# Where the second sums of a pair of groups are kept, and the order of one period's transposes, splits and scaling

## The chip, the cores and the metric

The kernel runs on one core of a Trainium2 chip. The metric is the device time of one execution in microseconds (us). Before the change three runs gave 612.68, 611.83 and 611.43 us, a median of 611.83. TensorE is called PE here, VectorE DVE, ScalarE ACT, GpSimd POOL and SyncE SP, as in the profile.

## The reference

Retention (4 batches, 8 heads, 768 steps, 64 wide) is followed by a feed-forward block with a gate:

```python
for t in range(S):
    state = gamma * state + einsum('bhd,bhe->bhde', k[:, :, t], v[:, :, t])
    y[:, :, t] = scale * einsum('bhd,bhde->bhe', q[:, :, t], state)
x = y.transpose(0, 2, 1, 3).reshape(3072, 512)
h = x @ w_in                      # 512 -> 2048
g = h * erf(softplus(h))
out = g @ w_out                   # 2048 -> 512
```

q, k, v and the output are float32; w_in and w_out come as 64-bit numbers, which the kernel converts itself.

## The kernel before, in words

**Precision.** A product x·w of the feed-forward block is made of three products in a faster format: x and w are each split into a high part, a low part and a difference (`split`, L328, and `split_weights`, L314: one ACT operation for the high part, then two DVE operations for `lo` and `dif`). The three products go to two sums in two PSUM banks, a (from hi and lo) and b (from dif), and the result is (1 + 1/Z)·a − b/Z.

**Groups, units, bricks.** The 3072 tokens are 12 groups of 256; a group is two chunks of 128 steps. The 2048 hidden columns are 16 strips of 128. A *unit* of `pair_unit` (L740) multiplies one strip for two neighbouring groups, g and g + 1: 8 matmuls into bank a, then 4 into bank b (L748), 512 columns each. The four banks of the pool `ps_o` serve two units in turn, so a unit's banks are those of the unit before the last. A unit's result, here called a *brick* (128 x 512 numbers, 256 KB), is *evacuated* by its `put` (L756): for most units `together` (L337), which is one ACT operation (L339) that copies a, scaled, into a small buffer h, and one DVE operation (L340) that adds b to it; then POOL starts the transfer of h to DRAM (`HID2`). For the units of g in `APART` (g = 1 and 2: 4 + 8 = 12 bricks) the two sums stay apart: ACT copies a to h (L760) and b to a second small buffer `low` (L761), and POOL transfers each on its own, `low` to `HID3` (L762) and h to `HID2` (L765). The small buffers (`b2`, L95) are six, shared by h, `low`, the masked scores `am` and the outputs y; large ones (`b4`, L92) are 34 of 4 KB a partition, shared by nearly everything else.

**Periods.** After a start in which groups 0 and 1 are made, the loop at L1052 runs periods g = 2 to 12. In period g PE runs the units of pair g − 1 (six units in period 2, eight afterwards), and the retention of chunks 2g + 2 and 2g + 3 is woven in. Two joins stand between units: `begin` (L577: scores and the chunks' own state updates, on PE) and `results` (L616: queries times states and scores times values, on PE, then ACT copies to xT at L651). Between them `states` (L595) masks the scores (L603, into `am`) and adds up the states (L614) on DVE. After `results`, `crossed_sums` (L654) makes four short DVE sums (L660, L662), and `split_x` (L664) makes x_hi on ACT (L331), x_lo and x_dif on DVE (L332, L333).

**Preparation.** The generator `prepare(j)` (L548) has five steps for the chunks j and j + 1: transpose the keys on DVE (L560), scale the queries on DVE (L555), transpose them (L560 again), and then twice scale the values of one chunk, 8 ACT operations (L567). Its first step is taken in the period before. SP loads the keys and queries for it in 16 pieces each (`load_pair`, L149, L163); POOL loads values and keys in another layout (L147, L157).

**Order.** Every engine works through its own list in order. The lists follow the dictionaries in `period` (L988): a unit's matmuls are issued, then what the dictionary has for that place, then the unit's `put`. In period 3 (g == G2 + 1, L1004) `begin` stands ahead of unit 3 and `results` ahead of unit 5. On ACT and DVE, place 0 has three steps of `prepare(8)` with `hi_of(2)` (the high part of weight piece 2) between; place 1 the split of piece 2, `hi_of(3)` and the fifth step; place 2 the split of piece 3; place 3 the states. Piece 2 is wanted by units 4 and 5, piece 3 by units 6 and 7.

**Last stage.** `project` (L940) multiplies the gated bricks with w_out: 48 steps of 24 matmuls (L957). Bricks are loaded back by `load_hidden` (L866) in transfers of 512 KB; of those whose sums are apart the second sums come in `low` buffers (L879) and are added on DVE (`add_lows`, L893). Softplus (L898) and erf (L902) run on ACT, the gate's product on DVE (L912). Half-groups that are apart are loaded one step earlier than the others (L1086, L1090).

Of the kernel before, what the change touches and what calls it, by code (L numbers as in the profile page):

```python
# [13 lines left out]
F32 = mybir.dt.float32  # L14
# [3 lines left out]
AF = mybir.ActivationFunctionType  # L18
# [3 lines left out]
P = 128  # L22
C = 128
JPC = 4
GT = 256
# [19 lines left out]
Z = 2.0**-12  # L45
# [4 lines left out]
def kernel(  # L50
# [13 lines left out]
    nc = tc.nc  # L64
# [7 lines left out]
    n_ft = d_ff // P  # L72
    NPC = n_ft // 2
    DH = d_model // 2
    FIRST = JPC // 2 - 1
# [10 lines left out]
    scratch = ctx.enter_context(tc.tile_pool(name="scratch", bufs=1, space=bass.MemoryType.DRAM))  # L86
# [5 lines left out]
    def b4(name, shape, dtype=F32):  # L92
        return big.tile([P] + shape, dtype, name=name, tag="b4")

    def b2(name, shape, dtype=F32):  # L95
        return small.tile([P] + shape, dtype, name=name, tag="b2")

    def b8(name, shape, dtype=F32):
# [4 lines left out]
    HID = {  # L103
        g: scratch.tile([P, n, GT], F32, name=f"hid{g}") for g, n in ALONE.items()
    }
    HID2 = {
        g: scratch.tile([P, n_ft // 2, 2, GT], F32, name=f"hids{g}") for g in range(FIRST, NG - 1)
    }

    APART = (FIRST, FIRST + 1)  # L110
    HID3 = {g: scratch.tile([P, n_ft // 2, 2, GT], F32, name=f"hidl{g}") for g in APART}
    XR = []
    WOF = [scratch.tile([P, 2, d_model], F32, name=f"wof{n}") for n in range(NPC)]

# [222 lines left out]
    def together(to, a, b):  # L337

        nc.scalar.activation(to, a, AF.Copy, scale=1 + 1 / Z)  # L339
        nc.vector.scalar_tensor_tensor(to, b, -1 / Z, to, op0=ALU.mult, op1=ALU.add)  # L340
# [29 lines left out]
    for r in range(2):  # L370
        own = slice(r * D, (r + 1) * D)
# [176 lines left out]
    def prepare(j):  # L548


        for name, store, x in (("k", KT, KB[j]), ("q", QT, QB[j])):
            if name == "q":
                own = x.rearrange("p u (a d) -> p u a d", d=32)
                scale = kq_b[:, 1, :, j % NC : j % NC + 2].rearrange("p u c a -> p u (c a)")
                nc.vector.tensor_tensor(  # L555
                    own, own, scale[:, :, :, None].to_broadcast([P, HP, 8, 32]), op=ALU.mult
                )
                yield
            t = b4(name + "T", [HP, 2 * C])
            nc.vector.transpose(t.rearrange("p u t -> p (u t)"), x.rearrange("p u t -> p (u t)"))  # L560
            for i in range(2):
                store[j + i] = t[:, :, i * C : (i + 1) * C]
            yield
        for i in range(2):
            for h in range(H):
                x = V[j + i][:, h]
                nc.scalar.activation(x, x, AF.Copy, scale=kq_s[:, (j + i) % NC, 0, h : h + 1])  # L567
            yield
# [167 lines left out]
    def place_of(g, of):  # L736

        return int(of % 3 > min(g % 3, (g + 1) % 3))

    def pair_unit(g, ft):  # L740

        a, b = banks(g == NG - 2)
        n, u = divmod(ft, 2)
        at = sorted((g % 3, (g + 1) % 3))
        at = slice(at[0], at[1] + 1, at[1] - at[0])
        for to, parts in ((a, (0, 1)), (b, (2,))):
            for kk, i in itertools.product(range(n_k), parts):
                nc.tensor.matmul(  # L748
                    to,
                    W[n][i][:, kk * 2 * P + u * P : kk * 2 * P + (u + 1) * P],  # L750
                    XR[i][:, at, kk],
                    start=(kk == 0 and i == parts[0]),
                    stop=(kk == n_k - 1 and i == parts[-1]),
                )

        def put():  # L756
            h = b2("h", [2, GT])
            if g in APART:
                low = b2("low", [2, GT])
                nc.scalar.activation(h, a, AF.Copy, scale=1 + 1 / Z)  # L760
                nc.scalar.activation(low, b, AF.Copy, scale=-1 / Z)  # L761
                nc.gpsimd.dma_start(HID3[g][:, ft % 8], low)  # L762
            else:
                together(h, a, b)
            nc.gpsimd.dma_start(HID2[g][:, ft % 8], h)  # L765

        return put
# [61 lines left out]

    pair = load_pair(JPC + 2)  # L830
    prep = prepare(JPC + 2)
    a, b = JPC, JPC + 1
    during = {
# [30 lines left out]
    HID_, LOWS, E, G, WO = {}, {}, {}, {}, {}  # L864

    def load_hidden(n):  # L866

        if n >= NG * NU:
            return
        HID_[n] = b4("hid", [4, GT])  # L870
        g, i = divmod(n, NU)
        of = g if g % 2 == i // 2 else g - 1
        LOWS[n] = []
        if FIRST <= of < NG - 1 and (of != 1 or i == 3):
            src = HID2[of][:, i % 2 * 4 : i % 2 * 4 + 4, place_of(of, g)]
            for f in range(2) if of in APART else ():
                LOWS[n].append(b2("low", [2, GT]))
                at = i % 2 * 4 + 2 * f
                nc.sync.dma_start(LOWS[n][f], HID3[of][:, at : at + 2, place_of(of, g)])  # L879
        else:  # L880
            at = i * 4 if g < 2 else i % 2 * 4
            src = HID[g][:, at : at + 4]
        nc.sync.dma_start(HID_[n], src)
# [101 lines left out]

    LOADS = {4: (3, 4, 5, 6), 5: range(2, 8), 6: (0, 1, 4, 5, 6, 7), 7: (2, 3, 4, 5), 8: (1, 2, 3, 4)}

    def period(g, prep, next_prep):  # L988

        a, b = 2 * g + 2, 2 * g + 3  # L990
        one, two = partial(partial, unit), partial(partial, pair_unit)
        if g == G2:
            units = [one(g, 4), one(g, 5)] + [two(1, ft) for ft in range(12, 16)]
            return units, joined(1, 4, g), {
                0: [(split_weights, 6)],
                1: [(states, a), (states, b), (hi_of, 7)],
                2: [(split_weights, 7), (hi_of, 0)],
                3: [(split_weights, 0), (hi_of, 1)],
                4: [(crossed_sums, a), (crossed_sums, b), (split_x, a, 2)],
                5: [(split_weights, 1), (steps, next_prep, 1)],  # L1000
            }, range(4)
        if g < NG:
            units = [two(g - 1, ft) for ft in range(8 - 8 * (g % 2), 16 - 8 * (g % 2))]
        if g == G2 + 1:  # L1004
            return units, joined(3, 5, g), {
                0: [(steps, prep, 2), (hi_of, 2), (steps, prep)],
                1: [(split_weights, 2), (hi_of, 3), (steps, prep)],
                2: [(split_weights, 3)],
                3: [(states, a), (states, b)],
                5: [(crossed_sums, a), (crossed_sums, b), (split_x, a, 2)],  # L1010
                7: [(steps, next_prep, 1)],
            }, range(4)
        if g < NG - 2:
            return units, joined(2, 5, g), {
                0: [(steps, prep, 4)],
                1: [(convert, 2)],
                2: [(states, a), (convert, 1)],
                3: [(states, b), (convert, 1)],
                4: [(convert, 2 if g < 8 else 1)],
                5: [(crossed_sums, a), (crossed_sums, b)],  # L1020
                6: [(split_x, a, 2)],
                7: [(steps, next_prep, 1 if g < NG - 3 else 4), (convert, 1)],
            }, LOADS.get(g, ())
        if g == NG - 2:
            return units, joined(1, 3, g), {
                0: [(steps, prep, 4), (load_w_out, 0)],
                1: [(states, a), (load_w_out, 1)],
                2: [(states, b), (split_w_out, 0)],
                3: [(crossed_sums, a), (crossed_sums, b)],
                4: [(split_w_out, 1), (load_hiddens, 0)],  # L1030
                5: [(split_x, a, 2)],
                6: [(softplus, 0), (load_w_out, 2)],
                7: [(erf, 0), (gated, 0)],
            }, ()
        if g == NG - 1:
            return units, {}, {
                0: [(split_g, 0), (split_w_out, 2), (load_w_out, 3)],
                1: [(split_g, 1), (load_hiddens, 1)],
                2: [(split_w_out, 3)],
                3: [(softplus, 1), (load_w_out, 4)],  # L1040
                4: [(erf, 1)],
                5: [(split_w_out, 4), (load_w_out, 5)],
                6: [(gated, 1)],
                7: [(split_g, 2), (load_hiddens, 2)],
            }, ()
        return [one(NG - 1, n) for n in range(NPC // 2, NPC)], {}, {
            0: [(split_w_out, 5), (load_w_out, 6)],
            1: [(split_g, 3), (load_w_out, 7)],
            2: [(split_w_out, 6)],
        }, ()  # L1050

    for g in range(G2, NG + 1):  # L1052
# [19 lines left out]
        prep = next_prep  # L1072
    split_w_out(7)

    for n in range(NG * NU):
        g, i = divmod(n, NU)
# [19 lines left out]
    for i in range(2):  # L1096
        at = slice(i * DH, (i + 1) * DH)
# [45 lines left out]
```

## Time and profile before

| | |
|---|---|
| median of three runs | 611.83 us |
| the profiled execution's own time | 612.2 us |
| its span, from first to last instruction | 610.5 us |
| granted TensorE clock | 0.999 |
| moved by DMA | 112.58 MB |

In the profile's rows the columns are as follows. The busy line has busy time, share of the span and number of instructions of each engine. A row of the windows view has the stretch, its length, then each engine's busy time and instructions, the granted clock, the mean share of 16 DMA engines that were busy, and GB/s. A row of the waits view has who waited, for whom, the total in us, how often and the longest. A row of a timeline has start and duration in us, engine, line, operation, the tiles written and read, shape, how many equal ones in a row, and in brackets how long the engine had been idle and what ended that. A row of groups has busy time and mean ns of one, then the idle time before and its enders. A row of the chain of work that ended last has start, duration, and what.

Period 3 begins near 100 us, the later ones follow every 26 us, and the last stage begins near 345 us.

### The profile page before, as it was taken

To read this page: it belongs to the slowest core of one execution; us is meant where nothing else is said; L and a number is where in the kernel's file an instruction comes from. 1 tells how busy PE (TensorE), PEld (TensorE's weight loads), DVE (VectorE), ACT (ScalarE), POOL (GpSimd) and SP (SyncE) were. 2 spreads that over 40 slices of the span, in tenths; PEclk is the share of its full clock that TensorE was granted. 3 is DMA by queue.
4 is the path that set the end of the run, shared out by engine and by line. 5 is a ranking of instruction groups with operands and counts; after the bars stand their busy time and mean duration, and the time that the engine had idled before them with its cause. 6 is when DMAs were issued, how large, how long until landed. Compare 5 with 4: busy or idle time off the path is not lost.

```text
span 610.5 us, 13200 instructions
## 1 busy us (share of the span) xinstructions
PE 602.3 (99%) x5190; PEld 504.7 (83%) x5190; DVE 461.4 (76%) x578; ACT 396.0 (65%) x625; POOL 138.8 (23%) x236
## 2 busy tenths in 40 slices
PE   8999999999999999999999999999999999999997
PEld 7888897888888888888888988888888888888885
DVE  5899897677978679787778986977877768668640
ACT  3684576474453634345486787889989888988910
POOL 1086545463526535241112200000000000000000
PEclk9999999999999999999999999999999999999999
DMA  9999689998979998894645865355424433531301
GB/s 203 313 257 280 169 170 276 284 252 241 223 198 272 279 269 169 253 231 151 225 152 183 288 205 177 100 172 173 130 74 141 144 98 104 172 124 48 105 34 35
DMA packets 148878, 112.58 MB, mean 184 GB/s; under 512 B 103376, under 2 KB 128208, under 8 KB 148816
## 3 DMA queue, kind: packets, MB, share of 16 engines
q1 hardware_dynamic: 132192, 61.24, 39.1%
q0 software_dynamic: 16064, 50.36, 25.9%
q8 instruction: 41, 0.67, 0.5%
q14 instruction: 21, 0.17, 0.1%
q10 hardware_dynamic: 560, 0.14, 0.1%
HBM read 72.89 MB, written 38.80 MB: 183 GB/s over the span
## 4 chain that ended last, share of the span: by engine, by line
PE 80%; DMA 9%; SPq 7%; DVE 2%; issue 1%; POOL 0%; DVEq 0%
PE o L748 29%; PE o L957 21%; PE r L957 11%; PE hp L957 11%; SPq L163 4%; DMA raw<-in_moe_w_in_dram 3%; DMA kb<-in_k_dram 2%; DMA qb<-in_q_dram 2%; SPq L199 2%; DMA hidl<-low 1%; PE o L721 1%; SPq L140 1%; PE hp L748 1%; PE r L748 1%; PE hp L583 1%
## 5 line engine op out<-in xcount | busy, mean ns | idle before, releaser
L748 PE MATMUL o<-x_hi,w_hi 128*128 128x512 f32 x288 | 114.3, 397 | 0.8 <-ACT h L760 0.8
L748 PE MATMUL o<-x_lo,w_lo 128*128 128x512 f32 x288 | 112.3, 390 | 0.3 <-DVE x_lo L332 0.3
L912 DVE TENSOR_TENSOR e<-hid,e 128x1024 f32<-128x1024 f32 x48 | 56.6, 1221 | 50.3 <-ACT e L902 50.2
L339 ACT ACTIVATE h<-o 128x512 f32<-128x512 f32 x64 | 37.7, 594 | 81.5 <-PE o L748 76.3
L748 PE MATMUL o<-x_dif,w_dif 128*128 128x512 f32 x288 | 77.0, 389 | 0.0
L765 POOL DMA_DIRECT2D hids<-h x76 | 41.9, 552 | 117.0 <-DVE h L340 110.0
L340 DVE SCALAR_TENSOR_TENSOR h<-o,h 128x512 f32<-128x512 f32 x64 | 43.7, 687 | 30.2 <-ACT h L339 27.5
L748 PEld LDWEIGHTS o<-x_hi,w_hi 128*128 128x128 f32 x288 | 54.0, 188 | 13.2 <-ACT h L760 1.2
L748 PEld LDWEIGHTS o<-x_lo,w_lo 128*128 128x128 f32 x288 | 54.1, 188 | 11.3 <-DVE x_lo L332 0.6
L748 PEld LDWEIGHTS o<-x_dif,w_dif 128*128 128x128 f32 x288 | 54.1, 188 | 11.2
L333 DVE SCALAR_TENSOR_TENSOR g_dif<-g_hi,g_lo 128x1024 fp32r<-128x1024 f32 x48 | 58.8, 1225 | 3.2
L331 ACT ACTIVATE g_hi<-e 128x1024 fp32r<-128x1024 f32 x48 | 51.0, 1062 | 15.6 <-DVE e L912 13.0
L332 DVE TENSOR_TENSOR g_lo<-e,g_hi 128x1024 fp32r<-128x1024 f32 x48 | 58.6, 1221 | 0.0
L898 ACT ACTIVATE e<-hid 128x1024 f32<-128x1024 f32 x48 | 48.5, 1053 | 4.2 <-DVE hid L893 2.9
L687 PE MATMUL hp<-xT,w 128*128 128x256 f32 x224 | 49.7, 381 | 0.0
L902 ACT ACTIVATE e<-e 128x1024 f32<-128x1024 f32 x48 | 48.2, 1052 | 0.3
L687 PEld LDWEIGHTS hp<-xT,w 128*128 128x128 f32 x224 | 42.1, 190 | 5.7
L957 PE MATMUL o<-w_hi,g_hi 128*128 128x512 f32 x120 | 46.7, 389 | 0.0
L957 PE MATMUL o<-w_lo,g_lo 128*128 128x512 f32 x120 | 46.7, 389 | 0.0
L957 PE MATMUL o<-w_dif,g_dif 128*128 128x512 f32 x120 | 46.7, 389 | 0.0
L567 ACT ACTIVATE v<-v,kq_s 128x64 f32<-128x64 f32 x144 | 35.6, 337 | 0.0
L898 ACT ACT_TABLE_LOAD x24 | 30.8, 1283 | 2.1 <-DMA hid<-hids 1.4
(208 smaller groups left out, 1274.9 us busy)
## 6 DMA issues: line engine op xcount, KB each, us to landing
hids<-h POOLq DMA_DIRECT2D x76, 256.0 KB, 4.2
hid<-hids SPq DMA_DIRECT2D x38, 512.0 KB, 5.4
raw<-in_moe_w_in_dram SPq DMA_DIRECT2D x32, 256.0 KB, 5.4
raw<-in_moe_w_out_dram POOLq DMA_DIRECT2D x32, 256.0 KB, 6.1
out_dram<-y SPq DMA_DIRECT2D x23, 256.0 KB, 2.1
hid<-hid SPq DMA_DIRECT2D x10, 512.0 KB, 5.2
kb<-in_k_dram SPq DMA_DIRECT2D x144, 32.0 KB, 3.3
v<-in_v_dram POOLq DMA_DIRECT2D x18, 256.0 KB, 6.4
```

The source lines that it names most:

```text
L331: nc.scalar.activation(hi, x, AF.Copy, scale=KEEP)
L332: nc.vector.tensor_tensor(lo, x, hi.bitcast(F32), op=ALU.subtract)
L333: nc.vector.scalar_tensor_tensor(dif, hi.bitcast(F32), Z, lo.bitcast(F32), op0=ALU.mult, op1=ALU.subtract)
L339: nc.scalar.activation(to, a, AF.Copy, scale=1 + 1 / Z)
L340: nc.vector.scalar_tensor_tensor(to, b, -1 / Z, to, op0=ALU.mult, op1=ALU.add)
L687: nc.tensor.matmul(HP_[bank][:, col], w[:, kk, ft % 2 * P : (ft % 2 + 1) * P], XC[g][:, kk], start=(kk == 0), stop=(kk == n_k - 1),)
L748: nc.tensor.matmul(to, W[n][i][:, kk * 2 * P + u * P : kk * 2 * P + (u + 1) * P], XR[i][:, at, kk], start=(kk == 0 and i == parts[0]), sto ...
L765: nc.gpsimd.dma_start(HID2[g][:, ft % 8], h)
L898: nc.scalar.activation(E[n], HID_[n], AF.Softplus)
L902: nc.scalar.activation(E[n], E[n], AF.Erf)
L912: nc.vector.tensor_tensor(E[n], HID_.pop(n), E[n], op=ALU.mult)
L957: nc.tensor.matmul(Y[g][t][x // 2], G[n][x][:, f, t * P : (t + 1) * P], W_OUT[ft // 2][x][:, ft % 2 * d_model : (ft % 2 + 1) * d_model], s ...
```

## The change

- `APART` holds only g = 1. Its four bricks (strips 12 to 15, made in period 2) put both sums in one large buffer of 4 KB a partition, which goes to DRAM in one transfer of 512 KB; `HID3` holds both sums side by side, and the last stage reads either from there.
- The eight units of g = 2 (period 3) are evacuated with `together`, like those of all later pairs; their bricks go to `HID2` and are loaded back without `low`.
- The values' scaling is a generator of its own, `values`. Only for j = 8 (`2 * JPC`) it is not the end of `prepare`, and in period 3 the order is: place 0: values of chunk 8, `hi_of(2)`; place 1: scaling and transpose of the queries, values of chunk 9; place 2: split of piece 2, `hi_of(3)`; place 3: the states, then the split of piece 3.

```diff
+    APART = (FIRST,)
+    HID3 = {g: scratch.tile([P, n_ft // 2, 2, 2, GT], F32, name=f"hid3_{g}") for g in APART}
     HID2 = {
         g: scratch.tile([P, n_ft // 2, 2, GT], F32, name=f"hids{g}") for g in range(FIRST, NG - 1)
+        if g not in APART
     }
-    APART = (FIRST, FIRST + 1)
-    HID3 = {g: scratch.tile([P, n_ft // 2, 2, GT], F32, name=f"hidl{g}") for g in APART}
...
+        if j != 2 * JPC:
+            yield from values(j)
+
+    def values(j):
         for i in range(2):
             for h in range(H):
                 x = V[j + i][:, h]
...
         def put():
+            if g in APART:
+                h = b4("h", [2, 2, GT])
+                nc.scalar.activation(h[:, 0], a, AF.Copy, scale=1 + 1 / Z)
+                nc.scalar.activation(h[:, 1], b, AF.Copy, scale=-1 / Z)
+                nc.gpsimd.dma_start(HID3[g][:, ft % 8], h)
+                return
             h = b2("h", [2, GT])
-            if g in APART:
-                low = b2("low", [2, GT])
-                nc.scalar.activation(h, a, AF.Copy, scale=1 + 1 / Z)
-                nc.scalar.activation(low, b, AF.Copy, scale=-1 / Z)
-                nc.gpsimd.dma_start(HID3[g][:, ft % 8], low)
-            else:
-                together(h, a, b)
+            together(h, a, b)
             nc.gpsimd.dma_start(HID2[g][:, ft % 8], h)
...
-            src = HID2[of][:, i % 2 * 4 : i % 2 * 4 + 4, place_of(of, g)]
+            four, own = slice(i % 2 * 4, i % 2 * 4 + 4), place_of(of, g)
+            src = HID3[of][:, four, 0, own] if of in APART else HID2[of][:, four, own]
...
-                nc.sync.dma_start(LOWS[n][f], HID3[of][:, at : at + 2, place_of(of, g)])
+                nc.sync.dma_start(LOWS[n][f], HID3[of][:, at : at + 2, 1, own])
...
+    vals = values(2 * JPC)
...
-                0: [(steps, prep, 2), (hi_of, 2), (steps, prep)],
-                1: [(split_weights, 2), (hi_of, 3), (steps, prep)],
-                2: [(split_weights, 3)],
-                3: [(states, a), (states, b)],
+                0: [(steps, vals), (hi_of, 2)],
+                1: [(steps, prep, 2), (steps, vals)],
+                2: [(split_weights, 2), (hi_of, 3)],
+                3: [(states, a), (states, b), (split_weights, 3)],
```

## The prediction, made before the result was known

> **What bounds the kernel now.** I read the page's busy line first, then the windows view, then who PE waited for.
>
> ```profile
> PE 602.3 (99%) x5190; PEld 504.7 (83%) x5190; DVE 461.4 (76%) x578; ACT 396.0 (65%) x625; POOL 138.8 (23%) x236
> ```
> ```profile
> 0.00:20.00 20.00, 17.07 (x208) 14.82 (x210) 12.90 (x28) 8.18 (x18) 2.44 (x15) 1.00 1.06 209
> 95.00:105.00 10.00, 8.94 (x38) 6.84 (x37) 5.65 (x8) 7.42 (x20) 4.59 (x8) 1.00 0.89 260
> 120.00:500.00 380.00, 380.00 (x3298) 316.77 (x3297) 299.46 (x368) 253.03 (x388) 83.08 (x134) 1.00 0.67 191
> 500.00:610.50 110.50, 106.46 (x470) 87.83 (x468) 63.58 (x59) 73.77 (x73) 0.00 (x0) 0.99 0.30 96
> ```
> ```profile
> PE o L748 <- ACT h L760: 0.8, 1, 0.8
> PE o L748 <- DVE x_lo L332: 0.3, 1, 0.3
> PE r L632 <- DVE state L614: 0.2, 1, 0.2
> ```
>
> TensorE bounds it. Of 8.2 us without a matmul, 2.9 lie in the first 20 us and 4.0 after the last matmul, which the change doesn't touch. The rest is one hole between 95 and 105 us and a short one at the states: just the stretch that the change rewrites. No matmul is removed or added, so the edit can win only what PE loses there, and can lose only by a new wait. Next, the PE timeline: first instructions of the units and joins of period 3, then (last two rows) the results step of period 6, which runs undisturbed.
>
> ```profile
> 94.24 0.50 PE L748 MATMUL o<-x_hi,w_hi 128*128 128x512 f32 x1
> 97.09 0.39 PE L748 MATMUL o<-x_hi,w_hi 128*128 128x512 f32 x1
> 100.75 0.49 PE L748 MATMUL o<-x_hi,w_hi 128*128 128x512 f32 x1 [0.78 <-ACT h L760]
> 104.15 0.39 PE L748 MATMUL o<-x_hi,w_hi 128*128 128x512 f32 x1
> 106.87 0.39 PE L748 MATMUL o<-x_hi,w_hi 128*128 128x512 f32 x1
> 109.69 0.69 PE L583 MATMUL hp<-qT,kT 64*64 64x64 f32 x32
> 111.71 0.50 PE L748 MATMUL o<-x_hi,w_hi 128*128 128x512 f32 x1
> 114.57 0.39 PE L748 MATMUL o<-x_hi,w_hi 128*128 128x512 f32 x1
> 117.38 0.72 PE L632 MATMUL hp<-qT,state 64*64 64x64 f32 x32
> 119.95 0.50 PE L748 MATMUL o<-x_hi,w_hi 128*128 128x512 f32 x1
> 196.56 0.69 PE L632 MATMUL hp<-qT,state 64*64 64x64 f32 x32
> 198.69 0.50 PE L748 MATMUL o<-x_hi,w_hi 128*128 128x512 f32 x1
> ```
>
> A unit of 12 matmuls takes 106.87 − 104.15 = 2.72 us (2.86 right after a join). The last two units of period 2 start at 94.24 and 97.09, so unit 0 of period 3 is due at 99.81. Unit 1 starts at 104.15, which puts unit 0 effectively at 101.43: **1.62 us lost**. The results step takes 119.95 − 117.38 = 2.57 us; undisturbed 198.69 − 196.56 = 2.13: **0.44 us lost**. Together 2.06 us. [...]
>
> Why it is lost: the waits of ACT and DVE between 84 and 125 us.
>
> ```profile
> ACT h L760 <- DMA hidl<-low: 8.8, 2, 7.7
> ACT h L760 <- DMA hid<-h: 2.6, 1, 2.6
> ACT low L761 <- DMA hid<-h: 2.3, 1, 2.3
> DVE am L603 <- DMA hidl<-low: 2.3, 1, 2.3
> ```
>
> These are waits for one of the six small buffers: each brick kept apart takes two of them until POOL's transfers land. Both engines work in order, so what stands behind is late too. ACT's timeline, then DVE's:
>
> ```profile
> 94.05 0.60 ACT L760 ACTIVATE h<-o 128x512 f32<-128x512 f32 x1 [2.62 <-DMA hid<-h]
> 96.97 0.60 ACT L761 ACTIVATE low<-o 128x512 f32<-128x512 f32 x1 [2.32 <-DMA hid<-h]
> 97.87 0.68 ACT L651 COPY xT<-r 128x256 f32<-128x256 f32 x2
> 99.16 1.06 ACT L331 ACTIVATE x_hi<-xT 128x1024 fp32r<-128x1024 f32 x1 [0.61 <-DVE xT L662]
> 100.12 0.58 ACT L760 ACTIVATE h<-o 128x512 f32<-128x512 f32 x1
> 102.98 2.02 ACT L567 ACTIVATE v<-v,kq_s 128x64 f32<-128x64 f32 x8
> ```
> ```profile
> 93.60 1.23 DVE L325 TENSOR_TENSOR w_dif<-w_hi,w_lo 128x1024 fp32r<-128x1024 f32 x1
> 98.58 0.48 DVE L662 TENSOR_TENSOR xT<-xT,r 128x128 f32<-128x128 f32 x2
> 100.25 1.22 DVE L332 TENSOR_TENSOR x_lo<-xT,x_hi 128x1024 fp32r<-128x1024 f32 x1 [1.19 <-ACT x_hi L331]
> 107.43 1.25 DVE L560 STREAM_TRANSPOSE qT<-qb 128x1024 f32<-128x1024 f32 x1
> 115.73 0.76 DVE L603 TENSOR_TENSOR am<-hp,causal_d 128x256 f32<-128x256 f32 x2 [2.30 <-DMA hidl<-low]
> 117.85 0.87 DVE L614 TENSOR_TENSOR state<-state,r 128x256 f32<-128x256 f32 x2
> ```
>
> Two held evacuations (94.05 and 96.97, in brackets how long and for whom) delay the copies of xT; these delay x_hi and x_lo; and behind x_hi stands the evacuation at 100.12 of the bank that unit 0 wants. DVE's masks (am, 115.73) wait for a small buffer as well, and the states behind them end at 118.72, when PE has been waiting for them. ACT's 7.7 us wait by itself costs PE nothing: no PE wait names it.
>
> **The change part by part.** *Big buffers for the four bricks.* By the built order, the four take slots of the pool of 34 whose last users (weight pieces, old x) are long done, so ACT waits for PE alone. The second evacuation of the brick ended by 92.5 runs at 92.55, the r copies follow the results step at 94.3 (it ends at 94.24). The four short sums on DVE, about 1.05 us, start when w_dif ends, 94.83, and end at 95.9; x_hi 96.0; x_lo, 1.09 us behind it as before, 97.1: 3.1 us earlier. The bricks of units 94.24 and 97.09 are evacuated by 98.1 and 100.6. Unit 0 then finds bank and x at 99.81: −1.62.
>
> *Group 2 without second sums.* Eight ACT operations, eight small transfers to DRAM and eight back go; eight adds of the last stage become eight operations of L340 in period 3.
>
> ```profile
> L340 DVE SCALAR_TENSOR_TENSOR h<-o,h 128x512 f32<-128x512 f32 x64 | 43.7, 687 | 30.2 <-ACT h L339 27.5
> L898 ACT ACT_TABLE_LOAD x24 | 30.8, 1283 | 2.1 <-DMA hid<-hids 1.4
> 410.62 21.76 PE o L957 x96
> ```
>
> That is 8 × 0.69 = 5.5 us more DVE work in 26 us, before the deadlines of qT and states. A bank's first half is released by ACT; the half that L340 reads is wanted only by a unit's ninth matmul, 1.8 us later.
>
> *The new order.* ACT: evacuations to 100.6, values 2.0, w_hi 1.05, unit 0's h at 103.4 to 104.0, second values to 106.0. DVE: x_lo to the key transpose is five operations of 1.2 us (seven from 100.25 to 108.68 before), done at 103.1; it then waits for h, L340 to 104.7, scaling and transpose of the queries to **107.1**. PE wants qT after unit 2, 99.81 + 3 × 2.72 = 107.97: 0.85 us to spare, the tightest place, uncovered if missed. Unit 1's L340 to 107.7, split 2 to 110.1 (wanted from 112.85), unit 2's to 110.7. The join's first part takes 2.02 us, to 109.99, so masks and states run 110.7 to 113.7 (3.0 us as from 115.73 to 118.72), with no transfer in front, since the small buffers are free; wanted from 107.97 + 2.02 + 2.86 + 2.81 = 115.66. So −0.44. Split 3 follows to 116.1, wanted after 120; the L340s to 117.3. After the results (117.79) the next x_dif comes near 122.7, for a unit due near 126. All queue behind the masks on DVE is thus early.
>
> *Queues.* POOL issues four transfers of 512 KB for eight of 256, and eight fewer after; its weight and value loads move up about 2 us. SP's next key pieces now wait for PE's use of qT in period 2 (done near 94; they started at 93.7), the query pieces for the second brick's landing. In the last stage four half-groups are loaded one step later, as the others are; a step is 21.76 / 4 = 5.44 us, and ACT's waits for such loads are 2.1 us in all, with no PE wait between 120 and 500. Adds, loads and order there: nothing, covered by PE; if ACT became late by a whole step, 5.4 us is the bound, but softplus runs four steps ahead of its matmuls.
>
> Sum: the profiled execution took 612.2 us (span 610.5 and 1.7 around it); 612.2 − 1.62 − 0.44 = **610.1**. The median shown is 0.4 lower, 611.8, and would give 609.8. I take 610.0.
>
> **Rivals.** *A, the third brick's landing gates DVE (slower).* Split 2's w_dif takes the big buffer of the third brick, so DVE waits for that transfer to land; L340, masks and states stand behind it.
>
> ```profile
> DMA to landing us min/median/max: 2.5/5.3/8.3
> ```
>
> That is for all 12 stores and 12 loads of second sums, 256 KB each. Issue is at 98.1; even two transfers' worth of the slowest, 16.6, gives 114.7. With landing at L the states end at L + 1.23 (w_dif) + 0.6 (L340) + 3.0 = L + 4.8. The results step wants the last of them only halfway through its 2.13 us, near 116.7, so nothing is lost up to L = 111.9 and 1 us per us after it: slower than before from 114.0, by 0.2% (1.2 us) from 115.2. If the transfers are served one behind the other at that pace, the second brick (93.1) lands at 109.7 and the third 8.3 later, at 118.0: 610.0 + 6.1 = 616.1. Against: both halves of a brick landed in parallel, and there is less traffic. [...]
>
> *B, only half of it.* PE's own waits name ACT and x_lo, so if x is late for another reason, only the states' 0.44 us is won: 611.7; if qT misses by about 0.9, 1.62 + 0.44 − 0.9 gives 611.0.
>
> *C, nothing arrives at the end.* The 2 us are given back later because a load or ACT doesn't move up: 611.8 to 612.2. Against: 380 us without a hole, with DVE and ACT at 79% and 67%.
>
> **How the numbers follow.** Forecast 0.70 (609.3 to 610.6, the runs before spread 0.4 below and 0.8 above their median), B 0.15, C 0.08, A 0.07. A measurement here tells about 0.2%, 1.2 us: faster means under 610.6. Faster 0.73 (forecast and a part of B), same 0.20, slower 0.07. The range 609.3 to 611.4 takes the forecast and most of B; A and most of C are left out.
>
> **What would show it.** Right: no PE wait between 95 and 120; unit 0's first matmul near 99.8, the join near 108.0, results near 115.7 and 2.1 long; ACT without waits for DMA; states with a margin of 2 us; everything after 120 shifted by 2.06. Wrong: a DVE wait on a brick's landing (A), PE waiting for qT or x_lo (B), a first PE wait after 126 (C).

## The result, and the profile after

The changed kernel took 610.54 us (median), the kernel before, run beside it, 612.15 us: a ratio of 0.9976, 95% interval [0.9965, 0.9986]. Measured again it took 610.39 us against 612.30, 0.9975 [0.9964, 0.9985]. The forecast was 610.0, its range 609.3 to 611.4. One of the ten executions of the first measurement, the one that was profiled, was disturbed (1796.58 us, with some 1000 ns for a matmul in place of 390), as was one of twelve of the kernel that sends each brick twice, further down (1012.28 us); the ratios leave both out, and the medians without them are 610.46 and 612.83. The profile below is that of the second measurement: 610.46 us, with a span of 608.4.

The busy line of the page, and the windows view (length, then busy time and instructions of each engine, PE's granted clock, the DMA engines' share and GB/s):

```profile
PE 602.5 (99%) x5190; PEld 505.8 (83%) x5190; DVE 461.8 (76%) x578; ACT 393.3 (65%) x617; POOL 130.7 (21%) x224
```
```profile
0.00:20.00 20.00, 18.05 (x214) 16.11 (x214) 12.80 (x28) 8.56 (x19) 2.45 (x15) 1.00 1.05 212
95.00:105.00 10.00, 10.00 (x46) 8.27 (x45) 7.62 (x10) 7.91 (x21) 3.39 (x5) 1.00 0.91 299
120.00:500.00 380.00, 380.00 (x3297) 316.75 (x3296) 296.06 (x359) 250.90 (x381) 79.22 (x127) 1.00 0.63 182
500.00:608.43 108.43, 104.40 (x461) 86.13 (x459) 63.59 (x59) 71.73 (x71) 0.00 (x0) 1.00 0.28 91
```

The hole between 95 and 105 is gone: PE is busy for all 10 us (8.94 before), and the 380 us from 120 on are as full as they were. Who PE waited for, in the whole span:

```profile
PE o L435 <- POOL ident masks.py:199: 1.5, 1, 1.5
PE r L483 <- ACT kqT L477: 0.3, 1, 0.3
```

Both rows belong to the start of the kernel; the three that named period 3 are gone. PE's timeline, the first instruction of the last two units of period 2, of the units 0, 1 and 2 of period 3, of the join, of units 3 and 4, of the results step and of unit 5:

```profile
94.05 0.50 PE L755 MATMUL o<-x_hi,w_hi 128*128 128x512 f32 x1
96.91 0.39 PE L755 MATMUL o<-x_hi,w_hi 128*128 128x512 f32 x1
99.63 0.39 PE L755 MATMUL o<-x_hi,w_hi 128*128 128x512 f32 x1
102.35 0.39 PE L755 MATMUL o<-x_hi,w_hi 128*128 128x512 f32 x1
105.07 0.39 PE L755 MATMUL o<-x_hi,w_hi 128*128 128x512 f32 x1
107.88 0.69 PE L590 MATMUL hp<-qT,kT 64*64 64x64 f32 x32
109.91 0.50 PE L755 MATMUL o<-x_hi,w_hi 128*128 128x512 f32 x1
112.76 0.39 PE L755 MATMUL o<-x_hi,w_hi 128*128 128x512 f32 x1
115.58 0.69 PE L639 MATMUL hp<-qT,state 64*64 64x64 f32 x32
117.79 0.50 PE L755 MATMUL o<-x_hi,w_hi 128*128 128x512 f32 x1
```

Unit 0 follows its forerunner after 99.63 − 96.91 = 2.72 us, the length of an undisturbed unit. The results step takes 117.79 − 115.58 = 2.21 us. ACT's timeline where it was held before, and DVE's masks and states:

```profile
94.17 0.65 ACT L658 COPY xT<-r 128x256 f32<-128x256 f32 x2 [0.39 <-PE r L650]
95.54 1.06 ACT L332 ACTIVATE x_hi<-xT 128x1024 fp32r<-128x1024 f32 x1 [0.72 <-DVE xT L669]
96.50 0.58 ACT L766 ACTIVATE h<-o 128x512 f32<-128x512 f32 x1
98.92 0.60 ACT L766 ACTIVATE h<-o 128x512 f32<-128x512 f32 x1 [1.22 <-PE o L755]
```
```profile
110.38 0.75 DVE L610 TENSOR_TENSOR am<-hp,causal_d 128x256 f32<-128x256 f32 x2
112.49 0.87 DVE L621 TENSOR_TENSOR state<-state,r 128x256 f32<-128x256 f32 x2
```

No wait of ACT in these rows is for a DMA any more; the copies of xT that stood at 97.87 start at 94.17. The masks start at 110.38 with no wait ahead of them (115.73 before, after 2.30 us of waiting), and the states end at 113.36, 2.2 us before PE wants them.

**Where the time went.** A way to compare all the kernels below: cut the profiled execution at two instructions that every one of them has, the x_dif matmuls of the last unit but one of period 2 (near 96 us) and those of unit 5 of period 3 (near 120). The change can move only what is between, the *stretch*. These are the rows of the kernel before at the units ahead of unit 0, at unit 0, at unit 4 and at unit 5, from its PE timeline, with the first row of the stretch on top:

```profile
96.19 1.07 PE L748 MATMUL o<-x_dif,w_dif 128*128 128x512 f32 x4
98.91 1.07 PE L748 MATMUL o<-x_dif,w_dif 128*128 128x512 f32 x4
103.25 1.07 PE L748 MATMUL o<-x_dif,w_dif 128*128 128x512 f32 x4
116.38 1.07 PE L748 MATMUL o<-x_dif,w_dif 128*128 128x512 f32 x4
121.89 1.07 PE L748 MATMUL o<-x_dif,w_dif 128*128 128x512 f32 x4
```

The same rows of the changed kernel:

```profile
96.00 1.07 PE L755 MATMUL o<-x_dif,w_dif 128*128 128x512 f32 x4
98.72 1.07 PE L755 MATMUL o<-x_dif,w_dif 128*128 128x512 f32 x4
101.44 1.07 PE L755 MATMUL o<-x_dif,w_dif 128*128 128x512 f32 x4
114.58 1.07 PE L755 MATMUL o<-x_dif,w_dif 128*128 128x512 f32 x4
119.74 1.07 PE L755 MATMUL o<-x_dif,w_dif 128*128 128x512 f32 x4
```

The stretch fell from 25.70 to 23.74 us: 1.62 at unit 0 (4.34 to 2.72) and 0.35 at the results (5.51 to 5.16). What lies ahead of it is 0.19 shorter, what follows up to the end of the span 0.05 longer (spans are taken to 0.1 us). "Around" is the time minus the span, that is what the device time holds before the first and after the last instruction. In the kernel before it was 1.70, in the changed kernel 2.06. Sum: 612.2 − 1.96 − 0.19 + 0.05 + 0.36 = 610.46. The table has the profiled executions with this cut, in us (two kernels that are some 11 and 28 us slower are left to their own paragraphs); the last column is the median of all runs, with its ratio to the kernel before as run beside it (whose median was 611.5 to 612.5).

| kernel | ahead | unit 0 | results | stretch | after it | around | median, ratio and interval |
|---|---|---|---|---|---|---|---|
| before | 96.2 | 4.34 | 5.51 | 25.70 | 488.6 | 1.70 | 612.15 |
| changed | 96.0 | 2.72 | 5.16 | 23.74 | 488.7 | 2.06 | 610.39, 0.9975 [0.9964, 0.9985] |
| buffers alone | 96.0 | 2.72 | 5.51 | 24.09 | 489.2 | 1.80 | 610.74, 0.9974 [0.9964, 0.9984] |
| order alone | 95.8 | 4.17 | 5.61 | 25.64 | 488.8 | 1.69 | 612.07, 0.9999 [0.9988, 1.001] |
| four bricks, small buffers | 96.0 | 3.78 | 5.02 | 25.37 | 489.7 | 1.82 | 612.27, 1.0003 [0.9993, 1.0013] |
| four big, eight small | 96.7 | 2.72 | 6.16 | 24.73 | 488.9 | 1.68 | 611.56, 1.0001 [0.9992, 1.001] |
| none apart | 96.0 | 2.72 | 5.06 | 24.70 | 488.7 | 1.67 | 611.19, 0.9988 [0.9979, 0.9996] |
| twelve big, old order | 95.7 | 2.72 | 12.19 | 30.76 | 488.6 | 1.92 | 616.34, 1.0071 [1.0059, 1.0083] |
| twelve big, new order | 96.2 | 2.72 | 5.04 | 29.11 | 489.5 | 1.84 | 617.24, 1.0079 [1.006, 1.0097] |
| each brick sent twice | 96.3 | 2.72 | 4.99 | 23.56 | 491.6 | 1.66 | 612.94, 1.0015 [1.0003, 1.0027] |
| second sums cut to a quarter | 95.9 | 3.70 | 5.78 | 25.34 | 488.5 | 1.77 | 612.13, 1.0001 [0.9991, 1.0012] |

The times of one kernel differ by a microsecond and more to either side from one execution to the next (610.85 to 614.59 us for the kernel before, beside the second measurement), and not in the stretch alone. Where the effect is under 1 us, the stretch of a single profile tells where time was won, and the median whether it is left at the end.

### The profile page after: what moved, and what is told of

Read it like the earlier page. It is cut to its first block, busy times and chain, and to the rows that moved or that the text cites. A ratio compares the mean times of both kernels' runs of the same rounds, so it can differ in the third digit from the quotient of the medians.

```text
span 1794.6 us, 13153 instructions
## 1 busy us (share of the span) xinstructions
PE 1789.1 (100%) x5190; PEld 1082.3 (60%) x5190; DVE 469.5 (26%) x578; ACT 395.1 (22%) x617; POOL 129.7 (7%) x224
## 4 chain that ended last, share of the span: by engine, by line
PE 100%; POOL 0%; DVE 0%; DVEq 0%; issue 0%; POOLq 0%
PE o L755 36%; PE o L965 19%; PE hp L694 10%; PE r L965 10%; PE hp L965 10%; PE o L728 2%; PE r L590 1%; PE r L639 1%; PE r L650 1%; PE r L597 1%; PE hp L755 1%; PE hp L590 1%; PE r L755 1%; PE hp L597 1%; PE hp L650 1%; PE r L483 1%
## 5 line engine op out<-in xcount | busy, mean ns | idle before, releaser
L755 PE MATMUL o<-x_lo,w_lo 128*128 128x512 f32 x288 | 294.1, 1021 | 0.0
L755 PE MATMUL o<-x_hi,w_hi 128*128 128x512 f32 x288 | 289.4, 1005 | 0.0
L755 PE MATMUL o<-x_dif,w_dif 128*128 128x512 f32 x288 | 236.7, 1001 | 0.0
L694 PE MATMUL hp<-xT,w 128*128 128x256 f32 x224 | 185.4, 1104 | 0.0
L755 PEld LDWEIGHTS o<-x_dif,w_dif 128*128 128x128 f32 x288 | 117.3, 407 | 98.4 <-issue 98.4
L755 PEld LDWEIGHTS o<-x_lo,w_lo 128*128 128x128 f32 x288 | 117.2, 407 | 96.9 <-issue 96.9
L755 PEld LDWEIGHTS o<-x_hi,w_hi 128*128 128x128 f32 x288 | 111.7, 388 | 89.7 <-issue 81.1
L694 PEld LDWEIGHTS hp<-xT,w 128*128 128x128 f32 x224 | 97.2, 436 | 81.2 <-issue 80.1
L965 PE MATMUL o<-w_hi,g_hi 128*128 128x512 f32 x120 | 99.6, 830 | 0.0
L965 PE MATMUL o<-w_lo,g_lo 128*128 128x512 f32 x120 | 99.6, 830 | 0.0
```

The source lines that it names most:

```text
L694: nc.tensor.matmul(HP_[bank][:, col], w[:, kk, ft % 2 * P : (ft % 2 + 1) * P], XC[g][:, kk], start=(kk == 0), stop=(kk == n_k - 1),)
L755: nc.tensor.matmul(to, W[n][i][:, kk * 2 * P + u * P : kk * 2 * P + (u + 1) * P], XR[i][:, at, kk], start=(kk == 0 and i == parts[0]), sto ...
L965: nc.tensor.matmul(Y[g][t][x // 2], G[n][x][:, f, t * P : (t + 1) * P], W_OUT[ft // 2][x][:, ft % 2 * d_model : (ft % 2 + 1) * d_model], s ...
```

## The experiments

**The changed kernel again**, for a profile to set beside that of the kernel before.

> The changed kernel once more, for an undisturbed profile. If the small buffers were the cause: no wait of PE between 95 and 120 us, unit 0 of period 3 starts near 99.8, the results step near 115.7 and 2.1 long, ACT waits for no DMA there; span 608.4 (610.5 - 2.06), 1.6 to 2.0 us under the kernel before. If only half was won (B): a wait of PE for qT or x_lo of 0.5 us or more is left in that stretch.

It took 610.39 us; its profile is the one above.

**Which part pays: the buffers alone.** The changed kernel with period 3 as it was:

```diff
-                0: [(steps, vals), (hi_of, 2)],
-                1: [(steps, prep, 2), (steps, vals)],
-                2: [(split_weights, 2), (hi_of, 3)],
-                3: [(states, a), (states, b), (split_weights, 3)],
+                0: [(steps, prep, 2), (hi_of, 2), (steps, prep)],
+                1: [(split_weights, 2), (hi_of, 3), (steps, prep)],
+                2: [(split_weights, 3)],
+                3: [(states, a), (states, b)],
```

> The changed kernel with the order of period 3 as it was (query transpose before the values' scaling, both splits ahead of the states). If the buffers are the cause and the order is only a margin: DVE then has qT near 105.5 and the states near 115.2, both before PE wants them (108.0 and 116.7), so it is within 0.3 us of the changed kernel. If the order earns a part: slower than the changed kernel by 0.4 to 1 us, with PE waiting at the results step for the states behind both splits and three evacuations.

610.74 us, 0.9974 [0.9964, 0.9984], level with the changed kernel. In the stretch the buffers alone win 1.61 of 1.96 us, all of it at unit 0. The results step stayed as long as before (5.51), though DVE had the states done at 114.5, a microsecond ahead, and no PE wait is shown there. The trace places the loss all the same: not at the states, where the kernel before lost it, but among the products of masked scores and values. Here is that row in this kernel, then in the changed one:

```profile
116.05 0.99 PE L649 MATMUL hp<-am,v 64*64 64x64 f32 x32
116.09 0.69 PE L650 MATMUL hp<-am,v 64*64 64x64 f32 x32
```

These 0.30 us are one pause between two of the 32 matmuls, which nothing in the profile ends; its cause isn't known, and no run ties it to the old order. So the stretch lacks 0.35 us of the changed kernel's gain; the time doesn't, since the changed kernel loses about as much around the span. Nothing here shows that the new order wins anything.

**The order alone**, in the kernel before (the reverse edit: the new dictionary and the separate generator `values`, with buffers and bricks as before).

> The kernel before with the new order of period 3 alone, twelve bricks apart in small buffers. If the buffers are the cause: both losses stay (unit 0 late by 1.6 us, masks waiting for a small buffer), within 0.4 us of the kernel before. If the order earns the gain: 610.2 to 610.9.

612.07 us, 0.9999 [0.9988, 1.001]. Both losses stay, with the same waits: the order by itself is worth 0.06 us in the stretch.

**Four bricks, but in small buffers.** The kernel before with `APART = (FIRST,)` and nothing else changed: the bricks of group 2 are summed, those of group 1 still take two small buffers each.

> The kernel before with only the four bricks of g = 1 apart, still in two small buffers each, old order. If the two losses have separate causes as predicted: unit 0 still starts 1.6 us late (the four bricks of period 2 are as before), but the masks find a small buffer, so about 0.4 us under the kernel before. If dropping the eight pairs of group 2 is what earns the gain: 1.6 to 2 us under it. If the whole loss sits in the four bricks' buffers: no change.

612.27 us, 1.0003 [0.9993, 1.0013]: my expectation of a small gain was missed. ACT still waits for the transfers of two earlier bricks, 3.4 us until 94.65 and 1.0 us until 96.22 (the row of the second wait names PE, whose matmuls had ended by 92.4; the transfer landed at 96.12), so unit 0 still loses 1.06 us; and the eight sums that now fall to DVE in period 3 come on top of a DVE that is late already, so unit 2 loses 0.57 more (its bank b is read late). The results step is free of its loss (5.02).

**Big buffers for four, the other eight as before.** In the kernel with the buffers alone (the loads of the last stage are changed to match and left out here):

```diff
             h = b2("h", [2, GT])
-            together(h, a, b)
+            if g == FIRST + 1:
+                low = b2("low", [2, GT])
+                nc.scalar.activation(h, a, AF.Copy, scale=1 + 1 / Z)
+                nc.scalar.activation(low, b, AF.Copy, scale=-1 / Z)
+                nc.gpsimd.dma_start(HIDL[:, ft % 8], low)
+            else:
+                together(h, a, b)
             nc.gpsimd.dma_start(HID2[g][:, ft % 8], h)
```

> Edit: the changed kernel's big buffers and single transfers for the four bricks of period 2, but the eight of period 3 keep two sums in small buffers with two transfers, as before; period 3 in its old order. Theory (the two gains hang together: unit 0 starts on time, but DVE's masks still wait for the small buffer of period 3's first brick, which landed at 115.65 us in the kernel before): the states end near 118, up to 1 us sooner since that brick is made 1.6 us sooner, while PE now wants them at 115.7 to 116.7: 1 to 2 us lost there in place of 0.4, so 611.0 to 612.0 us, with a wait of TensorE for the state and one of DVE for the second sum's transfer. Rival (the two gains are separate): 1.6 less than before, 610.5 to 610.7, the loss at the states still about 0.4.

Its waits: PE's after 90 us, and the longest of DVE between 84 and 126.

```profile
PE hp L639 <- DVE state L621: 0.2, 1, 0.2
PE r L639 <- DVE state L621: 0.2, 1, 0.2
```
```profile
DVE am L610 <- DMA hidl<-low: 4.6, 1, 4.6
```

Unit 0 is on time, and 6.16 − 5.03 = 1.13 us are lost at the results instead (5.03 is about what the step takes where nothing holds it, 4.99 to 5.06 in four kernels): the masks still wait for the second sum of period 3's first brick, and PE comes to them earlier. The time was 611.56 us against 611.55 before, ratio 1.0001; the 0.97 us that the stretch won are not seen in the medians (the interval, from 0.9992, leaves room for 0.5), and in the profile 0.5 of them are lost ahead of it and 0.3 behind it, for no reason that is known. Waits in a row behave like this here: what one gives back, the next takes. With the four bricks alone mended, half of the gain is left in the stretch, and none is shown in the time.

**No brick apart.** The changed kernel with `APART = ()`: the four bricks are summed on ACT and DVE as well.

> Edit: the changed kernel with no brick apart; the four bricks of period 2 are summed on ACT and DVE into one small buffer and one transfer of 256 KB each, like the rest. Theory: DVE gets 4 x 0.69 = 2.8 us more before x_lo of period 3, which ended at 97.8 us with 1.8 us to spare, so unit 0 waits about 1 us: 611.4 us, against 610.4 of the changed kernel. Rival 1 (order and buffers have slack, sums apart aren't needed at all): 610.4 or less and no TensorE wait near 99.6. Rival 2 (DVE is what two sums relieve by the whole of its work): unit 0 waits 2.8 us, 613.2 us.

611.19 us, 0.9988 [0.9979, 0.9996]: the theory's 611.4 to 0.2 us, but by another wait, so the agreement is chance. The theory had unit 0 wait about 1 us for x_lo; unit 0 is on time, and PE stops once in unit 1, for the bank b that DVE empties:

```profile
PE o L755 <- DVE h L341: 0.8, 1, 0.8
```

Two sums apart relieve DVE just where it is busiest (for 10.83 of the 11 us from 84 to 95 in this run); for the four bricks that is worth 0.96 us of the stretch.

**Twelve bricks in big buffers**, first in the old order, then in the new one: `APART = (FIRST, FIRST + 1)` in the kernel with the buffers alone, and in the changed kernel.

> Edit: all 12 bricks of periods 2 and 3 keep their two sums apart, each in one big buffer with one transfer; period 3 in its old order. Theory (what pays is that no brick holds a small buffer): as the changed kernel with the old order, 610.7 us, within 0.5, TensorE's waits for x_lo and for ACT near 97 us gone, and ACT without waits for DMA there. Rival (few bricks pay, since eight more with two sums take big buffers that the weights' splits want, or load ACT with 8 operations more): masks or splits wait for a transfer between 104 and 118 us, and 611.3 us or more.

> Edit: all 12 bricks of periods 2 and 3 in big buffers with one transfer each, as in the run that took 616.3 us, but with the changed kernel's order of period 3. In that run split 3 on DVE, ahead of masks and states, took the buffer of period 3's first brick, which landed at 116.2 us. Here, by the built order, ACT's w_hi of split 3 takes that buffer, at about 106 us, ahead of the next bricks' copies; DVE's part of split 3 stands behind the states. Theory (whichever split meets a brick still under way is held, so only four bricks may take big buffers): ACT waits near 106 us for a transfer for 8 to 10 us, TensorE for ACT or the states, 615 to 620 us. Rival (the new order lets twelve bricks pass, since the states no longer stand behind split 3): 610.5 to 611.5 us, no wait of TensorE between 95 and 120.

616.34 and 617.24 us, 1.0071 [1.0059, 1.0083] and 1.0079 [1.006, 1.0097]. My theory for the first (as good as four) fell, and the mechanism of the rival that I priced at 616.1 in the prediction came true in another kernel: a split takes the buffer of a brick whose transfer is under way. That 616.34 lies so near 616.1 is chance: that sum was for another brick, and the lowered clock shown at the end was not in it. The longest waits of DVE and of PE in the old order:

```profile
DVE w_lo L325 <- DMA hid<-h: 9.2, 1, 9.2
```
```profile
PE hp L638 <- DVE state L620: 4.7, 1, 4.7
```

The same of ACT and PE in the new order:

```profile
ACT w_hi L312 <- DMA hid<-h: 7.9, 1, 7.9
```
```profile
PE o L755 <- ACT h L766: 3.7, 1, 3.7
```

In both, period 3's first brick lands at 115 to 116 us, 9.8 us after its issue in the old order and 8.2 in the new one, behind loads of keys, values and weights in POOL's queue (in the kernel before POOL issued these from 103.62 to 107.70, and that brick's transfers from 107.70 on). In the old order DVE's w_lo of split 3 wants that buffer ahead of the masks; in the new one the states stand ahead of it, but ACT's w_hi of split 3 has the buffer, ahead of two evacuations. It isn't the order that makes twelve too many, but how long period 3's bricks are under way; period 2's land in time.

**How long may the four take?** The changed kernel with each brick sent first to a spare DRAM tensor, once and three times:

```diff
+                nc.gpsimd.dma_start(SPARE[:, ft % 4], h)
                 nc.gpsimd.dma_start(HID3[g][:, ft % 8], h)
```

> Edit: the changed kernel; each of the four bricks is also sent to a spare DRAM tensor, ahead of its own transfer, so that its big buffer comes free one transfer of 512 KB later. In the changed kernel the bricks landed at 98.6, 100.6, 102.5 and 105.2 us, some 2.0 us apart where they stood behind each other. Theory: the third lands near 108.4 us, under the 111.9 from which the prediction has DVE's masks late: no TensorE wait, 610.4 us, within 0.4. Rival (the third brick's landing has no slack): 612.4 to 616, with a DVE wait on a brick's transfer.

> Edit: as the last, but each of the four bricks is sent to the spare tensor three times ahead of its own transfer. At 2.0 us a transfer the third brick lands near 120 us. Theory (landing gates split 2's w_dif on DVE, and masks and states behind it, 1 us lost per us after 111.9): TensorE waits some 8 us at the results step near 116 us: 618 us, DVE's wait being on a brick's transfer. Rival 1 (the buffers of the bricks aren't on the way of anything in period 3): 610.4 to 611. Rival 2 (what stands behind in the queue, the value and weight loads and the next bricks' small buffers, comes late first): a loss of some us with ACT or PE waiting for those, not DVE for a brick.

Once: PE has no wait at all in the stretch (23.56), with the third brick landing at 106.7 us instead of 102.5: the landing has some 4 us to spare at the least. But the time was 612.94 us, 1.0015 [1.0003, 1.0027], which neither side foresaw: it lies in the rival's range, but without the rival's wait. All PE waits after 90 us:

```profile
PE o L756 <- issue: 1.2, 1, 1.2
PE r L651 <- issue: 1.1, 1, 1.1
```

They lie at 138 and 298 us, far from the bricks, and in both PE waited for nothing that the profile shows. What causes them wasn't tried. Three times: 640.55 us, 1.0453 [1.0436, 1.0471], much more than the 618 expected. The waits of qT, w_dif and w_hi for bricks ended at 110.1, 122.6 and 131.7 us, 12.4 and 9.1 us apart, where four transfers at 2.0 us would make 8; so the third brick landed at 131.6 and not near 120. Why the sends took longer is not shown. ACT stands still as well:

```profile
ACT w_hi L313 <- DMA hid<-h: 25.5, 1, 25.5
ACT h L341 <- DMA hids<-h: 15.7, 1, 15.7
```

The first row is the theory's kind of wait (a split for a brick's landing), the second Rival 2's (small buffers behind them in the queue). DVE's w_dif, which the theory named, waited 9.5 us for a brick as well, and qT 4.5 us. PE's largest waits were for ACT's evacuations, 19.1 us in all, and not at the results step. Both were right in part; the size was not.

**Is it the landing?** In the kernel before, second sums cut to a quarter of their columns (in transfer, load and addition); the result lacks the other three quarters. The transfer, as one of three such edits:

```diff
-                nc.gpsimd.dma_start(HID3[g][:, ft % 8], low)
+                nc.gpsimd.dma_start(HID3[g][:, ft % 8, :, : GT // 4], low[:, :, : GT // 4])
```

> Edit: the kernel before, in which each second sum is sent to DRAM, loaded back and added for the first quarter of its columns only, 64 KB instead of 256 (three quarters of the second sums are left out of the result). Buffers, copies and order stay. The bricks landed at 98.2 and 98.9 (first), 101.1 and 102.8 us (second). Theory (the loss is the time until the small buffers' transfers have landed): at 2.0 us per 512 KB each second sum lands some 0.7 us sooner, the first small buffers come free near 97.5 and the loss at unit 0 falls by 0.7 to 1.4: 610.8 to 611.5 us. Rival (not the landing but the copies, adds or number of transfers cost): 612.1, as before.

The loss at unit 0 falls from 1.62 to 0.98 us, by 0.64 and so just under the 0.7 to 1.4 us expected, since ACT's second wait ends at 96.01 and not at 96.97. But that wait is for the transfer of an earlier brick (L732), which the edit leaves at 256 KB. From issue to landing it took 6.5 us in the kernel before, 5.9 here, and 5.4 to 6.6 in kernels where no transfer was made smaller; so it isn't shown that the cut brought the landing forward. What speaks for the landing as the cause is how unit 0 follows it. The four kernels with the four bricks in small buffers, with the end of ACT's second wait counted from the first row of the stretch, in us:

| kernel | end of the wait | unit 0 |
|---|---|---|
| before | 0.78 | 4.34 |
| order alone | 0.61 | 4.17 |
| four bricks, small buffers | 0.19 | 3.78 |
| second sums cut to a quarter | 0.13 | 3.70 |

Unit 0 stands 3.56 to 3.59 us behind the end of that wait in all four, whatever moved the landing. In the changed kernel the same transfer lands no sooner (0.71 us after the first row, against 0.67 in the kernel before), and unit 0 is on time: the large buffers don't hasten the transfer, they keep ACT from having to wait for it.

Yet the results step grows to 5.78, as with the eight small ones above, and the median (612.13 us, 1.0001 [0.9991, 1.0012]) shows nothing.

**Another queue.** In the kernel before, the 24 transfers issued by ACT (`nc.scalar.dma_start`) instead of POOL.

> Edit: the kernel before, in which the 24 transfers of the 12 bricks with two sums are issued by ACT, right behind the two copies, and not by POOL, where they stand behind loads of weights and values and land 6 to 7.6 us after issue near 92 and 108 us. Buffers, copies, sums and order stay. Theory (the small buffers' release is the whole loss): they land 2 to 3.5 us after issue, ACT and DVE no longer wait for them, both losses go: 610.0 to 610.7 us. Rival 1 (an issue takes ACT as long as POOL, 0.55 us, 13 us in all in 45): copies of xT and evacuations come late, 612.3 or more. Rival 2 (it is the second copies and sums that cost): 612.1, as before.

623.45 us, 1.0191 [1.0159, 1.0224]: the theory and Rival 2 missed it, and Rival 1's open bound (612.3 or more) holds it by another cause. ACT's timeline (ACTq: its issues), and the largest of its waits:

```profile
112.50 0.58 ACT L761 ACTIVATE low<-o 128x512 f32<-128x512 f32 x1
121.64 0.33 ACTq L762 DMA_DIRECT2D hidl<-low  x1
```
```profile
ACT h L760 <- DMA qb<-in_q_dram: 11.3, 2, 10.4
```

The issue itself takes 0.33 to 0.45 us here, less than the 0.55 that I feared. But ACT's copy to low had ended at 113.08, the issue of its transfer started only at 121.64, 8.56 us later, and the next at 123.10. The evacuation behind them (123.47), which reads and writes nothing of the queries, had been idle for 10.39 us, and the profile puts that wait down to the landing of a piece of the queries, which SP had queued. Why ACT's issues stood still until then is not shown. So the run says nothing on the landing.

## Why the prediction was right

- **What bounds the kernel**: right. PE's loss was one hole and a long results step in period 3, and filling them shortened the span by about as much (2.1 us); after 120 us nothing changed.
- **Big buffers, −1.62**: right to the hundredth (4.34 to 2.72 us at unit 0), and by the path that was given: no DMA wait on ACT, copies of xT at 94.2, x_hi at 95.5, unit 0 at 99.63. The run with the buffers alone has the same. The hundredth is owed to reading the loss in the very execution that the result is compared with: other kernels with small buffers lost 0.98 to 1.45 us there, as the landing fell.
- **Results, −0.44**: 0.35 measured. The masks came at 110.4 to 113.4 as said (110.7 to 113.7), without a transfer ahead. The step takes 2.21 us and not 2.13. The run with eight bricks still in small buffers shows that the masks' wait was real and would have grown to 1.1 us. The new order is not shown to win anything: the old one had the states ready as well, its step lost 0.30 us in a pause at another place, and the times are level.
- **qT, the tightest place**: done at 106.9 (107.1 said), and the join at 107.88 had no wait.
- **"1.7 around it"**: the term that was mis-sized. I took it as fixed; it is 1.97 to 2.16 in every run of the changed kernel and 1.66 to 1.84 in every run of the kernel before. These 0.35 us are as much as the whole distance between 610.1 and 610.46; the other deviations (0.10 less won in the stretch, 0.19 won ahead of it, 0.05 lost behind it) cancel but for 0.04. The buffers alone have 1.74, none apart in the new order 1.75: neither part brings it by itself, and the cause stays open.
- **Rival A** was rightly held unlikely: the third brick landed at 102.5 us, where 111.9 was the limit. The four bricks' transfers, from issue to landing:

```profile
DMA to landing us min/median/max: 3.1/5.9/7.3
```

  So my bound (16.6) was wide; only the last brick took 3.1 us, and its forerunner landed 0.4 us after its issue. The mechanism itself is real: with twelve bricks in big buffers it made the kernel 4.4 to 4.8 us slower than before. **B and C** didn't happen.

## What to carry to other kernels

When PE is busy for 99% of the span, an edit is worth what PE loses in the stretch that it rewrites: take the first instructions of neighbouring units from the timeline and compare their distance with an undisturbed pair. Here that gave 2.06 us, where 1.96 were won and the holes alone showed 1.2 (in the windows view of the kernel before 1.06 between 95 and 105 us and 0.16 between 115 and 120). Look for all the waits on one scarce resource in that stretch before pricing the first, for the next one can take what the first gives back (0.65 of 1.62 us with the four bricks alone mended: the results step grew from 5.51 to 6.16). A buffer that an outgoing transfer held came free here only at its landing (in the kernel before 6.5 us after the issue at 90.34, and ACT's copy into the buffer started at 96.97), so ask which engine takes that slot next and what stands behind it, and measure whether the landing is before or after.

## What the runs showed that was not expected

**A long wait of PE cost more than itself.** In the old order with twelve big bricks PE stood still for 4.7 us, up to 120.0. The windows view (PE's granted clock is the third number from the end):

```profile
115.00:117.00 2.00, 0.29 (x2) 0.00 (x0) 0.68 (x1) 0.00 (x0) 0.00 (x0) 1.00 1.05 400
119.00:121.00 2.00, 0.97 (x22) 0.84 (x26) 1.97 (x7) 0.00 (x0) 0.55 (x1) 0.50 1.08 297
121.00:123.00 2.00, 2.00 (x88) 2.00 (x83) 0.74 (x2) 0.48 (x2) 0.00 (x0) 0.50 0.54 160
125.00:127.00 2.00, 2.00 (x10) 1.63 (x9) 0.81 (x3) 1.45 (x2) 0.00 (x0) 1.00 0.41 65
```

The clock was halved from 118.1 to 124.9 us, and the results step took 4.1 us (120.0 to 124.1) in place of 2.2; with the matmuls behind it, 12.19 − 5.03 = 7.2 us were lost by the table. In the new order a stop of 3.7 us did the same, with matmuls at 0.63 us in place of 0.39 behind it; the clock was at half from 116.9 to 120.3. These are 6.8 and 3.4 us. The clock fell 2.8 and 3.8 us after PE's last matmul had ended, and was back 4.9 and 3.6 us after PE was at work again. After the 0.8 us of the kernel before and the stops of 1.2 and 1.1 us above, it stayed at 1.00. What sets these times is not shown.

**The time around the span differed from program to program**: 1.7 to 2.05 us among kernels that are nearly alike. **PE has stops that no engine ends**, of up to 1.2 us, at places that differ from kernel to kernel (138 and 298 us above; 0.3 us at 116 and at 296 with the buffers alone). Neither was traced to its cause.
